# Two attentions on one core: moving A's work between steps, the first score ahead of the parts of the maximum, and some copies to other engines

## The chip, the core and the metric

The kernel runs on one core of a Trainium2 chip. The core has a matrix engine (TensorE; its matmuls are PE in the profile, its weight loads PEld), a vector engine (VectorE, DVE), a scalar engine for pointwise functions (ScalarE, ACT), a general engine (GpSimd, POOL), and SyncE (SP), which here only issues DMAs. Each engine works through its own queue in order and waits on semaphores that other engines and DMAs raise. The program writes its matmul results to eight tiles of PSUM (banks) of 128 partitions by 512 floats: seven for general use and `po`. The metric is the device time of one launch in microseconds.

## The reference

Two independent attention layers on inputs of 2048 rows and 576 columns, with 32 heads of 18 columns each; their outputs stand side by side. A attends from each position to eight earlier ones at distances 0, 2, ... 14; B attends to all positions.

```python
qkv = (x @ wqkv).reshape(B, S, 3, H, Dh).transpose(2, 0, 3, 1, 4)
# A: W, dil = 8, 2
idx = pos[:, None] - (jnp.arange(W) * dil)[None, :]
logits = einsum("bhsd,bhswd->bhsw", q, k[idx]) * Dh ** -0.5   # -1e9 where idx < 0
o = einsum("bhsw,bhswd->bhsd", softmax(logits), v[idx])
a = o.transpose(0, 2, 1, 3).reshape(B, S, D) @ wo
# B
p = softmax(einsum("bhqd,bhkd->bhqk", q, k) * Dh ** -0.5)
b = einsum("bhqk,bhkd->bhqd", p, v).transpose(0, 2, 1, 3).reshape(B, S, D) @ wo
return concatenate([a, b], axis=-1)
```

## The kernel before

**Stages.** First come the projections of B and A (up to about 412 us), which go to DRAM scratch: `dqk` and `dv` for B, `da` for A. Then the main loop at the end of the function: `NG` = 8 groups of four heads, `NB` = 4 blocks of 512 queries, `NT` = 16 tiles of 128 keys. One (g, b, kt) is a step, 512 in all; a block takes 16 steps.

**A step of B.** For four heads `score` computes a score matmul (keys by queries, 56 rows: 54 for the products and two that subtract the row's maximum) into one of four banks, and ScalarE takes the exponential into `e`. Heads 0 and 2 (h = 0, 2 in the code's order 0, 2, 1, 3) use array rows 0 to 63, heads 1 and 3 rows 64 to 127, so matmuls of the two row groups can run side by side. `weigh` (L731) multiplies the exponentials of the step before with V into `po`; after the sixteenth tile `finish` copies `po` to `o` on ScalarE (L740), and the sums are inverted and multiplied in some steps later (`den`, `drec`, `rec`).

**The maximum.** The exact maximum of each score row must be known before its block is scored. It is computed by further matmuls, pieces of it spread over all steps: `maximum(r)` does one piece of 512 columns in row group r into a bank that VectorE reduces (L168); `parts_of_maximum` does two half pieces, one of each row group, into the two halves of one bank. Both write one bank, so the program orders them: an empty ScalarE instruction (L243) stands between the two:

```python
one = both[1][0][0](ps, *both[1][1], part)
between = nc.scalar.nop()
sync(between, one)
def other():
    (take, reduce), piece = both[0]
    sync(take(ps, *piece, part), between)
    reduce(ps, *piece, part)
```

In the loop the parts come first, `other` after the third score, whole pieces after the first and the last score. These matmuls and the sums of products share three banks (`rings["else"]`). A block's maxima, transposed and split by `turn`, `halve` and `place`, are loaded into its rows of `qs` (L195) before its first score; that score is the first to wait for those loads. `given` counts pieces; when all 2048 are given, steps hold scores only and V products go in pairs of steps (`paired`).

**A beside it.** A is cut into eight tiles of 256 positions, `local(j)`, j = 0 to 7, each with a list of (step, function) from step `A_FROM + GAP * j` = 10 + 54 j: `fetch` loads q, k, v (tiles `aq`, one buffer, and `akv`, two); nine `match` on POOL multiply and add up q and k (L868, L872), the last gives the logits `lg` (L875); `most` takes the maximum over the eight neighbours on VectorE in three steps (L886), `lower` subtracts it on POOL (L892), `exponents` is on ScalarE (L895), `total` and `inverses` on VectorE, `share` multiplies on POOL (L905), and nine `weighted` on POOL (L911 to L914) make the output, which `upper` and `rest` split and `put` stores to `dao`. `get` loads it back transposed, and `sums_of_a` multiplies with wo, in four products a tile: a product is appended to `inside` at a step given by `MADE` and is issued in the next step ahead of its last score. `beside` issues it in both row groups, with two pieces of the maximum between its matmuls (L1036). `producing` holds the steps that have a product.

**Orders.** `agenda` maps a step to functions; `due()` runs a step's at its end, so what a step issues stands in its engine's queue behind that step's scores. An engine that isn't waiting may run ahead of the steps: SP and POOL do.

**The tail.** In the last group B's own products with wo (`sum_of`, L1055 and L1056) run from `waiting` in nearly every step; `closing` ends the last block.

Of the kernel before, what the change touches and what calls it, by code (L numbers as in the profile page):

```python
# [10 lines left out]
AF = mybir.ActivationFunctionType  # L11
# [8 lines left out]
DH = 18  # L20
W = 8
# [21 lines left out]
GAP = 54  # L43

A_FROM = 10

MADE = ((88, 96, 112, 128), (144, 160, 176, 192), (201, 208, 224, 240), (250, 256, 272, 288),
        (304, 320, 336, 352), (361, 368, 384, 400), (412, 416, 432, 448), (466, 468, 475, 480))


def ap(t, *dims):
# [10 lines left out]
def two_attentions(ctx: ExitStack, tc, xa, wa, woa, xb, wb, wob, out):  # L62
# [5 lines left out]
    nc = tc.nc  # L68
# [184 lines left out]
    e_room = None  # L253
    counted = [-1]

    def score(g, b, kt, h, kind="scores"):

        assert (g, b) in placed
        qs, ks = sets[g % 3]
        p, r = divmod(h, 2)  # L260
        ps = bank(kind)
        at = slice(64 * r, 64 * r + 56)
        nc.tensor.matmul(ps, ks[at, p, 128 * kt : 128 * kt + 128], qs[at, b, p], start=True, stop=True)  # L263

        counted[0] += 1
        early = counted[0] % 8 < 6
        e = (e_room if early else work).tile([128, 512], F32, name="e", bufs=6 if early else 2)
        nc.scalar.activation(e, ps, AF.Exp, scale=SCALE)  # L268
        return e
# [466 lines left out]
    def finish(g, b):  # L736
        o = work.tile([128, 512], F32, name="o", bufs=2)
        if g == NG - 1 and b == NB - 1:
            return closing(b, o, work.tile([128, 512], F32, name="rec", bufs=1))
        nc.scalar.activation(o, po, AF.Copy)  # L740
        den = work.tile([128, 16], F32, name="den", bufs=2)
        rec = work.tile([128, 512], F32, name="rec", bufs=1)
        parts = []

        def room():
            if g == NG - 1 and b == 0:

                parts[:] = [ap(work.tile([128, 4, 128], F32R, name=f"at{i}", bufs=1), (1, 512)) for i in range(2)]
            else:
                n = work.tile([128, 2, 512], F32R, name="n", bufs=1)  # L750
                parts[:] = n[:, 0], n[:, 1], n
            return parts

        if g == NG - 1 and b > 0:
            return shortly(b, o, rec, *room()[:2])

        def store():
            if g < NG - 1:
                load(do[:, g, :, 512 * b : 512 * b + 512].rearrange("i p n -> p i n"), parts[2].bitcast(F32))
            else:  # L760
                plan(step, full(b, parts))

        for at, f in ((1, lambda: load(den, o[DH:128:32])),
                      (8, lambda: nc.vector.reciprocal(den, den)),
                      (9, lambda: load(drec[g, b].rearrange("i (p n) -> (i p) n", n=16), den)),
                      (13, lambda: load(rec, rows(drec[g, b], (512, 4), (0, 32), (1, 512)))),
                      (18, lambda: nc.gpsimd.tensor_mul(o, o, rec)),  # L767
                      (19, lambda: nc.gpsimd.tensor_copy(room()[0], o)),
                      (20, lambda: nc.gpsimd.tensor_sub(parts[1], o, parts[0])),
                      (26, store)):  # L770
            later(at, f)
# [47 lines left out]
    wo = {}  # L819

    producing = set()

    def load_wo(k, src, *pieces):

# [20 lines left out]
    def local(j):  # L845
# [34 lines left out]
        def over_window(op, name, n):  # L880

            if n == 0:
                st[name] = work.tile([128, W // 2, SUB], F32, name=name, bufs=1)
            t, half = st[name], W >> n + 1
            src = t if n else st["lg"]
            nc.vector.tensor_tensor(t[:, :half], src[:, :half], src[:, half : 2 * half], op=op)  # L886

        def most(n):
            over_window(ALU.max, "am", n)
# [56 lines left out]
        def sums_of_a(h):  # L946
            his, los = zip(*wo["a"])
            w = his[:4], los[:4], his[4], los[4]
            cols = slice(288 * h, 288 * h + 288)
            if h == 0:  # L950
                st["y"] = ys["a", j, st["n"]] = work.tile([128, D], F32, name="y", bufs=4)
            one, two = beside("scores", *(halves(r, 0, w, st["x"], cols, slice(0, 128), True) for r in range(2)))
            y = st["y"][:, cols]
            nc.scalar.activation(y, two, AF.Copy)
            behind_scores.append(lambda: nc.vector.tensor_add(y, one, y))

        pieces = [(33, lower), (35, exponents), (39, share), (60, upper), (61, rest), (64, lambda: put(0)), (66, lambda: put(1))]

        pieces[:0] = [(at, lambda f=f, n=n: f(n)) for f, ats in ((most, (31, 32, 33)), (total, (36, 37, 38)),
                                                                (inverses, (38, 39))) for n, at in enumerate(ats)]  # L960
        for c in range(DH // 2):
            pieces.append((5 + 5 * c // 2, lambda c=c: match(c)))
            pieces.append((39 + 5 * c // 2, lambda c=c: weighted(c)))

        for nm, at, apart in (("q", -18, 2), ("k", -10, 2)) if j else (("q", -9, 1), ("k", -5, 1)):
            pieces += [(at + apart * i, lambda nm=nm, i=i: fetch(nm, i)) for i in range(4)]
        pieces += [(16 + 2 * i, lambda i=i: fetch("v", i)) for i in range(4)]
        made = [p - A_FROM - GAP * j for p in MADE[j]]
        for n, ends in enumerate((made[:2], made[2:])):
            pieces.append((max(ends[0] - 8, made[1] + 1 if n else 0), lambda n=n: get(n)))  # L970
            for h in range(2):
                pieces.append((ends[h], lambda h=h: finished(h)))
                producing.add(A_FROM + GAP * j + ends[h] + 1)
            pieces.append((ends[1] + 6, lambda n=n: load(out[p0 + 128 * n : p0 + 128 * n + 128, :D], ys["a", j, n])))
# [69 lines left out]
    def sum_of(y, t, h, chunks, kind=None):  # L1044

        pos, cols = slice(128 * t, 128 * t + 128), slice(288 * h, 288 * h + 288)
        both = []
        for r in range(2):
            both.append([])
            for c, (hi, lo) in enumerate(chunks):  # L1050
                at = slice(64 * r, min(64 * r + 64, hi.shape[0]))
                whi, wlo = wo["b"][c]
                both[r] += [(a[at, pos], w[at, cols]) for a, w in ((hi, whi), (hi, wlo), (lo, whi))]
        one, two = beside(kind, *both)
        nc.vector.tensor_copy(y, one)  # L1055
        nc.vector.tensor_add(y, two, y)  # L1056

    def first(t, b, h):
# [81 lines left out]
    while step < ALL:  # L1140
# [2 lines left out]
        es = [None] * 4  # L1143

        whole = total - sum(given) > 1
        parts = bool(begun) or total - sum(given) > 3

        ps = bank() if inside and whole else None
        if parts:
            part = parts_of_maximum()  # L1150
        for h in (0, 2, 1, 3):

            if inside and h == 3:
                inside.pop(0)()
            es[h] = score(g, b, kt, h)
            if h == 0 and whole:
                maximum(1, ps)()
            if h == 1 and parts:
                part()
            if h == 3 and whole:  # L1160
                maximum(0)()
        for fs in (behind_scores, outside):
# [42 lines left out]
```

## Time and profile before

| | |
|---|---|
| median of 3 runs | 1619.34 us (1617.29 to 1619.95) |
| the profiled execution | 1616.82 us, span 1615.0 us, granted TensorE clock 0.997 |
| score matmuls (L263) | 2048, 567.3 us busy |
| matmuls of the maximum (L160) | 2536, 791.8 us busy |
| products with V (L731) | 4096, 537.9 us busy |
| reductions of the maximum (L168, VectorE) | 2048, 1286.0 us busy, mean 684 ns |
| exponentials of B (L268, ScalarE) | 2048, 1050.2 us busy, mean 607 ns |
| copies of block sums (L740, ScalarE) | 31, 19.5 us busy, mean 628 ns |

A row of groups gives line, engine, operation, output and inputs, shapes and count, then busy time in us, mean ns of one, idle time of the engine just before them and what ended it. A row of the timeline gives the start, the duration, engine, line, operation, tiles, shapes and count, and in brackets the idle time before it with its releaser. A row of windows gives the stretch, its length, then busy time and count for each engine, the granted clock and the DMAs. `x2` in the timeline means that two instructions are merged into one row; the duration is then that of both.

### The profile page before, as it was taken

To read this page: it belongs to the slowest core of one execution; us is meant where nothing else is said; L and a number is where in the kernel's file an instruction comes from. 1 tells how busy PE (TensorE), PEld (TensorE's weight loads), DVE (VectorE), ACT (ScalarE), POOL (GpSimd) and SP (SyncE) were. 2 spreads that over 40 slices of the span, in tenths; PEclk is the share of its full clock that TensorE was granted. 3 is DMA by queue.
4 is the path that set the end of the run, shared out by engine and by line. 5 is a ranking of instruction groups with operands and counts; after the bars stand their busy time and mean duration, and the time that the engine had idled before them with its cause. 6 is when DMAs were issued, how large, how long until landed. Compare 5 with 4: busy or idle time off the path is not lost.

```text
span 1615.0 us, 35230 instructions
## 1 busy us (share of the span) xinstructions
PE 1599.0 (99%) x13394; PEld 959.5 (59%) x13394; DVE 1393.9 (86%) x2366; ACT 1212.4 (75%) x2419; POOL 961.1 (60%) x792
## 2 busy tenths in 40 slices
PE   9999999999999999999999999999999999999998
PEld 7999888999544444444444444444444444445676
DVE  5199999999899998999999999999999999999532
ACT  6424442121799998999999999999999999998444
POOL 2405742210265995996995995995996997920000
PEclk9999999999999999999999999999999999999999
DMA  8937954432222262254235235332532241034201
GB/s 250 239 121 196 275 164 133 134 104 79 60 56 64 73 147 54 62 118 113 62 85 133 72 98 115 98 91 60 125 106 58 59 135 47 22 124 139 89 38 60
DMA packets 186058, 172.11 MB, mean 107 GB/s; under 512 B 119152, under 2 KB 132976, under 8 KB 184160
## 3 DMA queue, kind: packets, MB, share of 16 engines
q1 hardware_dynamic: 181024, 158.31, 35.3%
q0 software_dynamic: 4032, 10.63, 3.1%
q8 instruction: 105, 1.72, 0.5%
q10 hardware_dynamic: 832, 0.92, 0.2%
q14 instruction: 65, 0.53, 0.1%
HBM read 96.94 MB, written 71.90 MB: 105 GB/s over the span
## 4 chain that ended last, share of the span: by engine, by line
PE 82%; POOL 7%; DVE 5%; DMA 3%; ACT 2%; issue 1%; SPq 0%; POOLq 0%; DVEq 0%; ACTq 0%
PE po L731 24%; PE bank L160 15%; PE bank L353 15%; PE bank L263 15%; PE bank L1036 8%; PE bank L290 5%; DVE mx L168 4%; ACT e L268 2%; POOL pr L868 1%; POOL pr L872 1%; POOL pr L911 1%; DMA akv<-da 1%; DMA dqk<-olo 1%; POOL pr L912 1%; POOL pr L913 0%
## 5 line engine op out<-in xcount | busy, mean ns | idle before, releaser
L168 DVE TENSOR_REDUCE mx<-bank 128x2 f32<-128x512 f32 x2048 | 1286.0, 684 | 114.5 <-PE bank L160 86.2
L268 ACT ACTIVATE e<-bank 128x512 f32<-128x512 f32 x2048 | 1050.2, 607 | 90.3 <-PE bank L263 83.2
L160 PE MATMUL bank<-ks,qs 54*128 54x256 f32 (+1 forms) x2536 | 791.8, 377 | 7.4 <-DVE mx L168 5.9
L160 PEld LDWEIGHTS bank<-ks,qs 54*128 54x128 f32 x2536 | 411.3, 184 | 464.6 <-DVE mx L168 423.4
L263 PE MATMUL bank<-qs,ks 56*128 56x512 f32 x2048 | 567.3, 426 | 0.1
L731 PE MATMUL po<-e,v 128*19 128x512 f32 x4096 | 537.9, 599 | 0.0
L263 PEld LDWEIGHTS bank<-qs,ks 56*128 56x128 f32 x2048 | 299.3, 185 | 14.7 <-issue 7.5
L868 POOL TENSOR_TENSOR pr<-aq,akv 128x1024 f32<-128x1024 f32 x72 | 158.5, 2202 | 15.4 <-DMA akv<-da 12.8
L911 POOL TENSOR_TENSOR pr<-lg,akv 128x1024 f32<-128x1024 f32 x72 | 158.5, 2201 | 0.6
L872 POOL TENSOR_TENSOR pr<-pr 128x1024 f32<-128x1024 f32 x64 | 152.6, 2384 | 5.0
L731 PEld LDWEIGHTS po<-e,v 128*19 128x19 f32 x4096 | 70.5, 97 | 129.4 <-issue 127.0
L681 ACT ACTIVATE ohi<-bank 128x512 f32<-128x512 f32 (+1 forms) x56 | 30.4, 595 | 152.5 <-issue 100.7
L353 PE MATMUL bank<-xhi,ahi 64*128 64x512 f32 (+1 forms) x448 | 113.5, 387 | 0.0
L353 PE MATMUL bank<-xhi,alo 64*128 64x512 f32 (+1 forms) x448 | 112.3, 387 | 0.0
L353 PE MATMUL bank<-xlo,ahi 64*128 64x512 f32 (+1 forms) x448 | 111.9, 388 | 0.1
L912 POOL TENSOR_TENSOR pr<-pr 128x512 f32<-128x512 f32 x72 | 92.5, 1285 | 5.6
L401 POOL TENSOR_TENSOR alo<-raw,ahi 128x512 fp32r<-128x512 f32 (+1 forms) x14 | 17.6, 1258 | 120.7 <-ACT ahi L400 88.8
L493 POOL TENSOR_TENSOR olo<-olo,ohi 128x512 fp32r<-128x512 f32 x36 | 46.2, 1294 | 66.1 <-ACT ohi L492 57.5
L767 POOL TENSOR_TENSOR o<-o,rec 128x512 f32<-128x512 f32 x29 | 37.6, 1297 | 58.7 <-ACT e L268 34.2
L103 POOL CAST mh<-mt 128x32 fp32r<-128x32 f32 x32 | 6.9, 217 | 102.3 <-DVE mt L183 99.5
L353 PEld LDWEIGHTS bank<-xhi,ahi 64*128 64x128 f32 (+1 forms) x448 | 65.0, 181 | 2.9
L353 PEld LDWEIGHTS bank<-xhi,alo 64*128 64x128 f32 (+1 forms) x448 | 63.9, 182 | 2.9
(197 smaller groups left out, 1827.6 us busy)
## 6 DMA issues: line engine op xcount, KB each, us to landing
do<-n SPq DMA_DIRECT2D x28, 512.0 KB
da<-ohi SPq DMA_DIRECT2D x52, 256.0 KB
akv<-da SPq DMA_DIRECT2D x64, 175.5 KB
out<-y SPq DMA_DIRECT2D x32, 288.0 KB
qs<-dqk SPq DMA_DIRECT2D x30, 288.0 KB
ks<-dqk SPq DMA_DIRECT2D x30, 288.0 KB
at<-dao SPq DMA_DIRECT2D x64, 128.0 KB
rec<-drec SPq DMA_DIRECT2D x29, 256.0 KB
```

The costliest lines, as they stand in the source:

```text
L160: return nc.tensor.matmul(ps if part is None else ps[:, 256 * r : 256 * r + 256], qs[at, b, p, 128 * t : 128 * t + 128], ks[at, p, 512 * k ...
L168: nc.vector.tensor_reduce(at, ps.rearrange("q (s n) -> q s n", s=2), axis=AX.X, op=ALU.max)
L263: nc.tensor.matmul(ps, ks[at, p, 128 * kt : 128 * kt + 128], qs[at, b, p], start=True, stop=True)
L268: nc.scalar.activation(e, ps, AF.Exp, scale=SCALE)
L290: nc.tensor.matmul(ps, a, b, start=c == i == 0, stop=c == 4 and i == 1)
L353: nc.tensor.matmul(ps, a, b, start=start, stop=stop)
L731: nc.tensor.matmul(po[32 * i : 32 * i + 19], vs[g][:, kt, 19 * i : 19 * i + 19], es[i], start=kt == 0, stop=kt == NT - 1)
L868: nc.gpsimd.tensor_mul(pr, ap(st["q"][:, 2 * c], (SUB, 2), (0, W), (1, SUB)), window(st["k"], c))
L872: nc.gpsimd.tensor_add(st["pr"], st["pr"], pr)
L911: nc.gpsimd.tensor_mul(at, ap(st["lg"], (0, 2), (SUB, W), (1, SUB)), window(st["v"], c))
L912: nc.gpsimd.tensor_add(at[:, :, :4], at[:, :, :4], at[:, :, 4:])
L1036: nc.tensor.matmul(ps, a, b, start=start, stop=stop)
```

## The change

It has seven parts. (1) In a step the first score is issued ahead of the first part of the maximum (`between`). (2) `finish` copies `po` on VectorE where the next step has no product and maxima are left; the next step then does no parts. (3) `most` and `total` work in four pieces of at most 128 elements per partition; they, `exponents`, `share`, `weighted`, `upper`, `rest` and `put` move to steps up to four later (for j = 0 four earlier than that). (4) `exponents` is issued inside a product's step where one falls on its step. (5) For j > 0 the first three matches go 15 to 18 steps ahead of the tile's start, into the step range of the tile before, the other six one or two steps earlier than they were, and q and k are fetched earlier. (6) Products of `MADE` move by up to eight steps, `get` is two steps later ahead of a product. (7) `sum_of` copies on ScalarE where its banks are both of the ring of three, in the tail.

```diff
-MADE = ((88, 96, 112, 128), (144, 160, 176, 192), (201, 208, 224, 240), (250, 256, 272, 288),
-        (304, 320, 336, 352), (361, 368, 384, 400), (412, 416, 432, 448), (466, 468, 475, 480))
+MADE = ((96, 100, 112, 128), (144, 160, 176, 192), (201, 208, 224, 240), (256, 262, 272, 288),
+        (304, 320, 336, 352), (368, 370, 384, 400), (416, 424, 432, 448), (466, 468, 475, 480))
...
-    def score(g, b, kt, h, kind="scores"):
+    def score(g, b, kt, h, kind="scores", between=None):
...
         nc.tensor.matmul(ps, ks[at, p, 128 * kt : 128 * kt + 128], qs[at, b, p], start=True, stop=True)
+        if between:
+            between()
...
-        nc.scalar.activation(o, po, AF.Copy)
+        if step + 1 in producing or sum(given) == total:
+            nc.scalar.activation(o, po, AF.Copy)
+        else:
+            nc.vector.tensor_copy(o, po)
+            copied.add(step + 1)
...
-            t, half = st[name], W >> n + 1
-            src = t if n else st["lg"]
-            nc.vector.tensor_tensor(t[:, :half], src[:, :half], src[:, half : 2 * half], op=op)
+            at, size, apart = ((0, 2, 4), (2, 2, 4), (0, 2, 2), (0, 1, 1))[n]
+            t, src = st[name], st[name] if n > 1 else st["lg"]
+            nc.vector.tensor_tensor(t[:, at : at + size], src[:, at : at + size],
+                                    src[:, at + apart : at + apart + size], op=op)
...
             y = st["y"][:, cols]
+            while beside_product:
+                beside_product.pop()()
             nc.scalar.activation(y, two, AF.Copy)
...
-        pieces = [(33, lower), (35, exponents), (39, share), (60, upper), (61, rest), (64, lambda: put(0)), (66, lambda: put(1))]
-        pieces[:0] = [(at, lambda f=f, n=n: f(n)) for f, ats in ((most, (31, 32, 33)), (total, (36, 37, 38)),
-                                                                (inverses, (38, 39))) for n, at in enumerate(ats)]
-        for c in range(DH // 2):
-            pieces.append((5 + 5 * c // 2, lambda c=c: match(c)))
-            pieces.append((39 + 5 * c // 2, lambda c=c: weighted(c)))
-        for nm, at, apart in (("q", -18, 2), ("k", -10, 2)) if j else (("q", -9, 1), ("k", -5, 1)):
+        soon = 0 if j else 4
+        in_product = A_FROM + GAP * j + 36 - soon in MADE_IN
+        pieces = [(34, lower), (36, (lambda: beside_product.append(exponents)) if in_product else exponents),
+                  (43, share), (64, upper), (65, rest), (68, lambda: put(0)), (70, lambda: put(1))]
+        pieces[:0] = [(at, lambda f=f, n=n: f(n)) for f, ats in ((most, (31, 32, 33, 34)), (total, (38, 39, 40, 41)),
+                                                                (inverses, (42, 43))) for n, at in enumerate(ats)]
+        pieces += [(43 + 5 * c // 2, lambda c=c: weighted(c)) for c in range(DH // 2)]
+        pieces = [(at - soon, f) for at, f in pieces]
+        pieces += [(5 + 5 * c // 2 if not j else (-18, -17, -15)[c] if c < 3 else 11 + 5 * (c - 3) // 2, lambda c=c: match(c))
+                   for c in range(DH // 2)]
+        for nm, at, apart in (("q", -26, 2), ("k", -25, 2)) if j else (("q", -9, 1), ("k", -5, 1)):
...
-            pieces.append((max(ends[0] - 8, made[1] + 1 if n else 0), lambda n=n: get(n)))
+            pieces.append((max(ends[0] - 6, made[1] + 1 if n else 0), lambda n=n: get(n)))
...
-        nc.vector.tensor_copy(y, one)
+        if kind:
+            nc.vector.tensor_copy(y, one)
+        else:
+            nc.scalar.activation(y, one, AF.Copy)
         nc.vector.tensor_add(y, two, y)
...
-        parts = bool(begun) or total - sum(given) > 3
+        parts = (bool(begun) or total - sum(given) > 3) and step not in copied
         ps = bank() if inside and whole else None
-        if parts:
-            part = parts_of_maximum()
+        part = []
         for h in (0, 2, 1, 3):
...
-            es[h] = score(g, b, kt, h)
+            es[h] = score(g, b, kt, h, between=(lambda: part.append(parts_of_maximum())) if parts and h == 0 else None)
             if h == 0 and whole:
                 maximum(1, ps)()
             if h == 1 and parts:
-                part()
+                part[0]()
```

More of the change, by code (lines that the diff above doesn't have):

```diff
@@ L821, in two_attentions @@
     producing = set()
+    copied = set()
+    MADE_IN = {p for ends in MADE for p in ends}
+    beside_product = []
     def load_wo(k, src, *pieces):
```

## The prediction

> **What bounds the kernel now.** I read the page first, for the engines' shares and the chain that ended last, then a step of the main loop in the timeline, then windows over the loop.
>
> ```profile
> span 1615.0 us, 35230 instructions
> ...
> PE 1599.0 (99%) x13394; PEld 959.5 (59%) x13394; DVE 1393.9 (86%) x2366; ACT 1212.4 (75%) x2419; POOL 961.1 (60%) x792
> ...
> PE 82%; POOL 7%; DVE 5%; DMA 3%; ACT 2%; issue 1%; SPq 0%; POOLq 0%; DVEq 0%; ACTq 0%
> ```
>
> TensorE is on the path nearly everywhere. The chain also says that POOL is on it somewhere (7%). One ordinary step, with no product of A in it:
>
> ```profile
> 898.92 0.38 PE L160 MATMUL bank<-ks,qs 54*128 54x256 f32 x1
> 898.93 0.49 PE L263 MATMUL bank<-qs,ks 56*128 56x512 f32 x1
> 899.03 0.30 PEld L263 LDWEIGHTS bank<-qs,ks 56*128 56x128 f32 x2
> 899.15 0.40 PE L160 MATMUL bank<-ks,qs 54*128 54x512 f32 x1
> 899.26 0.52 PE L263 MATMUL bank<-qs,ks 56*128 56x512 f32 x2
> 899.41 0.18 PEld L160 LDWEIGHTS bank<-ks,qs 54*128 54x128 f32 x1
> 899.50 0.29 PE L160 MATMUL bank<-ks,qs 54*128 54x256 f32 x1
> 899.58 1.89 DVE L168 TENSOR_REDUCE mx<-bank 128x2 f32<-128x512 f32 x3 [0.18 <-PE bank L160]
> 899.96 1.05 PE L731 MATMUL po<-e,v 128*19 128x512 f32 x8
> 900.94 0.38 PE L160 MATMUL bank<-ks,qs 54*128 54x256 f32 x1
> ```
>
> The matmuls run in two row groups side by side: the first part of the maximum (898.92, 256 columns, group 1) with the first score (898.93, 512 columns, group 0), and so on; then the eight products with V (899.96), and the next step begins at 900.94, after 2.02 us. The reader should see a small wait in the middle. The second part (899.50) goes into the same bank as the first, so the program puts an empty ScalarE instruction (L243) between them: it waits for the first part, and the second part waits for it. The first part ends at 898.92 + 0.38 = 899.30; the weights of the second are loaded from 899.41, 0.11 later, while the weight loader has been idle since 899.33. So **each step already hangs on part 1, ScalarE, part 2**, at present almost for free, because row group 0 is busy with the score of 899.26 until about then.
>
> ```profile
> L243 ACTq EVENT_SEMAPHORE  x488: 17/17/17, 418.8 to 1504.8; - x163
> 700.90:727.35 26.45, 14.45 (x52) 7.70 (x52) 1.00 0.69 146
> 418.30:1498.00 1079.70, 546.90 (x1944) 288.49 (x1944) 1.00 0.34 89
> 418.30:1498.00 1079.70, 75.74 (x864) 69.69 (x864) 1.00 0.34 89
> 1264.10 0.38 PE L160 MATMUL bank<-ks,qs 54*128 54x256 f32 x1
> 1268.24 0.38 PE L160 MATMUL bank<-ks,qs 54*128 54x256 f32 x1
> ```
>
> The first row counts that instruction: 488 steps have one. The window rows are of the scores (L263, four a step) and of A's products (L1036, 27 matmuls each). 52 scores in 26.45 us is 2.035 us a step. A step with a product takes 1268.24 - 1264.10 = 4.14 us, 2.11 more. The loop from 418.30 to 1498.00 has 1944 / 4 = 486 steps and 864 / 27 = 32 products: 486 x 2.035 + 32 x 2.11 = 1056.5. It took 1079.7, so **23 us in it are stalls**: the most that better placing can win there. The rest is the rate of the step.
>
> **The change part by part.**
>
> *First score ahead of part 1.* No instruction is added. But the part is now the second matmul in TensorE's queue, behind a longer one in the other row group. If a matmul's signal leaves at its own end, that is free. If signals leave in program order, the part's can't come before the score's. One place of the trace tells, in the stage of the projections:
>
> ```profile
> 88.83 0.50 PE L160 MATMUL bank<-ks,qs 54*128 54x512 f32 x1
> 88.83 0.39 PE L353 MATMUL bank<-whh,xhl 64*128 64x288 f32 x1
> 89.40 0.29 ACT L571 ACTIVATE vs<-bank 128x144 f32<-128x144 f32 x1 [4.22 <-PE bank L160]
> ```
>
> ScalarE, idle for 4.22 us, waits only for the product whose last matmul is the short one (288 columns, done at 89.22). It starts at 89.40, 0.07 after the end of the long one that was queued ahead of it (89.33), and the view names the long one as releaser. An ordinary release takes 0.03 (899.15 + 0.40 to 899.58). So the short one's signal followed the long one's by some 0.04: program order.
>
> Here that means: part 1 signals not 0.38 us after the start, but at the score's 0.49 plus 0.04, that is 0.15 later. ScalarE's empty instruction, the weights of part 2 and all of TensorE behind them move by as much, since its queue is in order. Part 2 would start at 0.58 + 0.15 = 0.73. What follows it takes 900.94 - 899.50 = 1.44, and no less where it is late already:
>
> ```profile
> 449.42 0.38 PE L160 MATMUL bank<-ks,qs 54*128 54x256 f32 x1
> 449.78 0.47 PE L263 MATMUL bank<-qs,ks 56*128 56x512 f32 x1
> 450.32 0.28 PE L160 MATMUL bank<-ks,qs 54*128 54x256 f32 x1
> 451.75 0.38 PE L160 MATMUL bank<-ks,qs 54*128 54x256 f32 x1
> 452.21 0.63 ACT L740 ACTIVATE o<-po 128x512 f32<-128x512 f32 x1
> 456.27 0.38 PE L160 MATMUL bank<-ks,qs 54*128 54x256 f32 x1
> 1480.76 0.38 PE L160 MATMUL bank<-ks,qs 54*128 54x256 f32 x1
> 1481.16 0.46 PE L263 MATMUL bank<-qs,ks 56*128 56x512 f32 x1
> ```
>
> At 449.42 part 2 came 0.90 after part 1 and the next step began 451.75 - 450.32 = 1.43 after it: lateness of part 2 passes on whole. The new step is 0.73 + 1.43 = 2.16, 0.12 over 2.035. Bounds: nothing (own end) and 0.15 (no absorption). I take 0.12, as the row at 89.40 is of the same engine and the same pairing of row groups. The first score doesn't reach ScalarE earlier either: its exponential is queued behind the empty instruction. Number of steps: 488, less six that skip their part (below), and two late steps that get one back: 484 x 0.12 = **+58 us** (0 to 73).
>
> [...]
>
> The same edit also gains. At 449.42 and 1480.76, steps that open a new block of queries, the score starts 0.36 and 0.40 after the part instead of beside it, as it first waits for several loads into qs. With the score first, these waits run during the products with V before it. Of the 31 block openings about a dozen show it, the two rows being the first and last: 12 x 0.36 = -4.3.
>
> *VectorE copies the block sums.* The copy on ScalarE (452.21) stretches the two steps around it to 456.27 - 451.75 = 4.52, 0.45 over two plain ones. Six copies have no product behind them (steps 16 to 80 and 464). On VectorE it queues behind three reductions and the next V products wait for it: I leave 0.2 each, so -1.5 (0 to -2.7). The part that is skipped pays for the VectorE time; its six pieces of the maximum come back in steps 488 to 490, where two products then take pieces between their matmuls: some +0.6 there, which I set against fewer waits. 0.
>
> *A's chain, its matches and loads.*
>
> ```profile
> 622.61 0.43 DVE L886 TENSOR_TENSOR am<-lg 128x256 f32<-128x256 f32 x1 [3.38 <-POOL lg L875]
> 623.68 0.58 PE L160 MATMUL bank<-ks,qs 54*128 54x256 f32 x1 [2.85 <-DVE mx L168]
> 623.60:630.70 7.10, 7.01 (x45) 5.04 (x45) 5.25 (x11) 2.69 (x5) 0.00 (x0) 0.54 0.19 47
> L868 POOL TENSOR_TENSOR pr<-aq,akv 128x1024 f32<-128x1024 f32 x72 | 158.5, 2202 | 15.4 <-DMA akv<-da 12.8
> L872 POOL TENSOR_TENSOR pr<-pr 128x1024 f32<-128x1024 f32 x64 | 152.6, 2384 | 5.0
> L892 POOL TENSOR_TENSOR lg<-lg,am 128x512 f32<-128x512 f32 x8 | 10.3, 1282 | 38.8 <-DVE am L886 38.8
> L905 POOL TENSOR_TENSOR lg<-lg,as 128x512 f32<-128x512 f32 x8 | 10.2, 1279 | 60.3 <-DVE as L902 53.3 <-ACT e L268 7.1
> ```
>
> The one large stall is in the second tile: VectorE's maximum stood 3.38 us at POOL's logits, TensorE idled 2.85, and then ran 7.1 us at a granted clock of 0.54, which costs 7.1 x 0.46 = 3.3: 6 together. Three matches of the next tile cost 3 x 2.20 + 2 x 2.38 = 11.4 us of POOL and go into its idle time at the chain, (38.8 + 60.3) / 8 = 12.4 us a tile, so POOL comes to the logits earlier; and the first product moves from step 88 to 96, behind it in part. -6 (0 to -6). The chain's pieces of 256 elements (0.43) become two of half the size: a little more VectorE work, in smaller pieces over four more steps. The exponentials go beside a product in five of the eight tiles. For these and all other stalls 23 - 6 - 4.3 - 6 x 0.45 = 10 are left. By the new places alone I would give 1.5 of them back; with steps of 2.16 VectorE and ScalarE have 0.12 more in each step, and I leave 3.5: -6.5 (-9 to +2). The loads: q and k of the next tile are issued some 10 and 15 steps earlier. On SP they stand ahead of the sums' small loads and wait for POOL's last match to free aq; nothing on TensorE's path stands behind them within a few steps. 0. The fetch for a product is issued six steps ahead, not eight, and the tile's stores four steps later: 0 while it lands within six steps, 12 us (a rival below).
>
> *ScalarE in the tail.* There TensorE runs a product in every step:
>
> ```profile
> 1592.46 0.46 DVE L1055 COPY y<-bank 128x288 f32<-128x288 f32 x1 [3.55 <-PE bank L1036]
> 1592.69 2.07 ACT L268 ACTIVATE e<-bank 128x512 f32<-128x512 f32 x4 [0.32 <-PE bank L263]
> 1595.17 0.62 PE L731 MATMUL po<-e,v 128*19 128x512 f32 x4
> ```
>
> The copy is as long on ScalarE, and pushes the four exponentials by 0.2, to 1594.98, still before 1595.17. 0 (-1 to +2).
>
> **Sum** against the profiled execution (1616.8, span 1615.0): +58 - 4.3 - 1.5 - 6 - 6.5 = +40. A little of the gains is lost since the stalls no longer give the other engines time to catch up: +38. The median shown is 2.5 above that execution: 1619.3 + 38 = **1657**.
>
> **Rivals.**
> 1. *Signals leave at each matmul's own end.* Then part 1 signals at 0.38 as now, and the gains stand alone: -4.3 - 1.5 - 6, and only -1.5 of A's chain: -13, **1606**. For it: the row at 89.40 is a single place, of another stage. Against: the view names the long matmul as releaser there. It decides from a delay of part 2 under 13 / 484 = 0.03. Chance 0.11.
> 2. *The delay is mostly absorbed*, because steps wait in that time for other things anyway. Left 0.04 x 484 = 19, against 17 of gains: **1621**. Against: 1.43 after a late part 2. Chance 0.05.
> 3. *Forecast, and a product finds its data late* (tiles 4 and 7, whose products stay while the stores move back): a stall as at 623.68, some 6 us: **1663**. Chance 0.06; slower steps speak against it, as they leave the loads more time.
> 4. *The forecast*, **1657**: 0.78.
>
> **Numbers.** The per-step cost from 0.09 to 0.15 gives 44 to 73; the recovered stalls 14 to 24: 1639 to 1676. I take 1637 to 1678, which leaves out rivals 1 and 2. A measurement tells 0.2% (3 us) from no change: faster 0.11, same 0.05, slower 0.84.
>
> **What would show it.** Right: part 2 starts 0.73 after its step's first matmul, plain steps take 2.15 (52 scores in 28 us), the score of a new block starts with its step, no stall at the second tile, the clock near 1.0, shares of DVE and ACT lower over a longer span. Wrong: part 2 still at 0.58, then it is rival 1; part 2 at 0.73 but steps of 2.05, rival 2.

## The result and the profile after

The changed kernel took 1661.92 us (median of 4 runs, 1661.38 to 1662.10), the kernel before 1618.32 us beside it (4 runs, 1615.92 to 1619.95): a ratio of 1.0272, 95% interval 1.0255 to 1.0288. The forecast was 1657 (1637 to 1678). In the changed kernel the score is L263, its exponential L270, the products with V L733, A's products L1057, matches L879 and L883, the logits L886, VectorE's window operations L898, the share L918.

First the page of the kernel after: span, engines, the chain that ended last, and two groups, whose last columns are the idle time ahead of it and what ended it.

```profile
span 1660.0 us, 35220 instructions
...
PE 1648.0 (99%) x13390; PEld 943.0 (57%) x13390; DVE 1395.8 (84%) x2361; ACT 1231.4 (74%) x2440; POOL 962.0 (58%) x792
...
PE 93%; DVE 2%; DMA 2%; POOL 1%; issue 1%; SPq 1%; ACT 0%; POOLq 0%; ACTq 0%; DVEq 0%
...
L263 PEld LDWEIGHTS bank<-qs,ks 56*128 56x128 f32 x2048 | 304.4, 184 | 423.5 <-ACT e L270 415.6
...
L160 PEld LDWEIGHTS bank<-ks,qs 54*128 54x128 f32 x2532 | 398.2, 184 | 114.2 <-ACTq L243 99.5
```

On the page of the kernel before, the same two groups:

```profile
L160 PEld LDWEIGHTS bank<-ks,qs 54*128 54x128 f32 x2536 | 411.3, 184 | 464.6 <-DVE mx L168 423.4
...
L263 PEld LDWEIGHTS bank<-qs,ks 56*128 56x128 f32 x2048 | 299.3, 185 | 14.7 <-issue 7.5
```

VectorE and GpSimd work as long as before and ScalarE 19 us longer, in a span 45 us longer; the chain is nearly all TensorE's (93%, 82% before). The row of L160 names the new wait: 99.5 us in which the weight loader stood idle until ScalarE's empty instruction L243. (The idle time of some 420 us, 0.85 at the start of each step, while the products with V run, only changes rows, as the step now opens with the score.) One plain step in the timeline shows it:

```profile
897.59 0.50 PE L263 MATMUL bank<-qs,ks 56*128 56x512 f32 x1
...
898.23 0.18 PEld L160 LDWEIGHTS bank<-ks,qs 54*128 54x128 f32 x1 [0.22 <-ACTq L243]
898.23 0.39 PE L160 MATMUL bank<-ks,qs 54*128 54x256 f32 x1
...
899.75 0.49 PE L263 MATMUL bank<-qs,ks 56*128 56x512 f32 x1
```

The weights of the second part start 0.64 us after the step's first matmul (before: 899.41 - 898.92 = 0.49), and the step takes 899.75 - 897.59 = 2.16. The windows of the scores (stretch, length, busy time and count) give it for many steps, 52 scores and then the loop:

```profile
672.00:700.08 28.08, 14.72 (x52) 7.78 (x52) 1.00 0.09 30
418.50:1544.00 1125.50, 559.99 (x1944) 293.21 (x1944) 1.00 0.34 85
```

The first stretch holds 52 scores, 13 steps at 2.160 us. The loop's 486 steps took 1125.5 us, 45.8 more than before. 486 x (2.160 - 2.035) = +60.8; so the stalls shrank by 15.0. With 32 products at 2.11 (a step with a product still takes 2.10 us more than a plain one, 4.26 in the median), what is left in the loop beside the plain rate is 1125.5 - 486 x 2.160 - 67.5 = 8.2 us, where it was 23.

### The profile page after: what moved, and what is told of

Read it like the earlier page. It is cut to its first block, busy times and chain, and to the rows that moved or that the text cites. A ratio compares the mean times of both kernels' runs of the same rounds, so it can differ in the third digit from the quotient of the medians.

```text
span 1660.0 us, 35220 instructions
## 1 busy us (share of the span) xinstructions
PE 1648.0 (99%) x13390; PEld 943.0 (57%) x13390; DVE 1395.8 (84%) x2361; ACT 1231.4 (74%) x2440; POOL 962.0 (58%) x792
## 4 chain that ended last, share of the span: by engine, by line
PE 93%; DVE 2%; DMA 2%; POOL 1%; issue 1%; SPq 1%; ACT 0%; POOLq 0%; ACTq 0%; DVEq 0%
PE po L733 29%; PE bank L263 20%; PE bank L160 18%; PE bank L355 14%; PE bank L1057 7%; PE bank L292 5%; DVE mx L168 1%; DMA ks<-dqk 1%; POOL xlo L403 1%; DMA at<-dao 1%; DMA dqk<-olo 0%; DVE as L898 0%; SPq L143 0%; PE bank L507 0%; DMA more<-xa 0%
## 5 line engine op out<-in xcount | busy, mean ns | idle before, releaser
L270 ACT ACTIVATE e<-bank 128x512 f32<-128x512 f32 x2048 | 1061.7, 605 | 95.3 <-PE bank L160 40.1
L160 PE MATMUL bank<-ks,qs 54*128 54x256 f32 (+1 forms) x2532 | 836.2, 390 | 2.6 <-DVE mx L168 2.0
L263 PE MATMUL bank<-qs,ks 56*128 56x512 f32 x2048 | 581.5, 429 | 0.0
L263 PEld LDWEIGHTS bank<-qs,ks 56*128 56x128 f32 x2048 | 304.4, 184 | 423.5 <-ACT e L270 415.6
L733 PE MATMUL po<-e,v 128*19 128x512 f32 x4096 | 537.6, 599 | 0.2 <-DVE o L746 0.2
L160 PEld LDWEIGHTS bank<-ks,qs 54*128 54x128 f32 x2532 | 398.2, 184 | 114.2 <-ACTq L243 99.5
L879 POOL TENSOR_TENSOR pr<-aq,akv 128x1024 f32<-128x1024 f32 x72 | 158.3, 2203 | 53.4 <-DMA akv<-da 32.1
L883 POOL TENSOR_TENSOR pr<-pr 128x1024 f32<-128x1024 f32 x64 | 152.5, 2383 | 5.0
L733 PEld LDWEIGHTS po<-e,v 128*19 128x19 f32 x4096 | 70.5, 97 | 130.6 <-issue 125.2
L355 PE MATMUL bank<-xlo,ahi 64*128 64x512 f32 (+1 forms) x448 | 117.1, 388 | 0.1
L355 PEld LDWEIGHTS bank<-xlo,ahi 64*128 64x128 f32 (+1 forms) x448 | 67.4, 182 | 4.9 <-POOL xlo L403 0.5
```

The source lines that it names most:

```text
L160: return nc.tensor.matmul(ps if part is None else ps[:, 256 * r : 256 * r + 256], qs[at, b, p, 128 * t : 128 * t + 128], ks[at, p, 512 * k ...
L355: nc.tensor.matmul(ps, a, b, start=start, stop=stop)
L733: nc.tensor.matmul(po[32 * i : 32 * i + 19], vs[g][:, kt, 19 * i : 19 * i + 19], es[i], start=kt == 0, stop=kt == NT - 1)
L879: nc.gpsimd.tensor_mul(pr, ap(st["q"][:, 2 * c], (SUB, 2), (0, W), (1, SUB)), window(st["k"], c))
L883: nc.gpsimd.tensor_add(st["pr"], st["pr"], pr)
```

## The experiments

The theory: the step's lengthening is the late signal of part 1. A rival for the sum: the rest of the change costs something, too. The first four runs part them. "Score first alone" is the kernel before with `between` and nothing else; "part first again" is the kernel after without it.

```diff
 # e2, e4 against the kernel after (e4: only where kt == 0 and not 96 <= step < 368 is the score first)
-        part = []
+        part = [parts_of_maximum()] if parts else []
...
-            es[h] = score(g, b, kt, h, between=...)
+            es[h] = score(g, b, kt, h)
 # e3 against the kernel after, in steps that hold whole pieces and no product
-            if h == 1 and parts:
-                part[0]()
+            if h == 1: maximum(0)()      # it stood behind the fourth score
...
+        part[0]()                                      # behind the fourth score
+        rings["else"].append(rings["else"].pop(0))
```

> The kernel before with one thing of the change alone: the first score ahead of the first part of the maximum in every step. Theory (TensorE's signals leave in program order, so the part's signal now leaves behind the longer score's, and the second part, which waits for it through ScalarE's empty instruction, starts 0.12 to 0.13 us later in each of some 488 steps): 488 x 0.125 = +61 us, less the block-opening waits of some 4 us that go with it, so about 1675 us (1665 to 1682), plain steps of 2.16 us, and the stall of some 6 us in the second tile is still there. Rival (the rest of the change, A's chain and the copies, costs the time, and each signal leaves at its own end): 1605 to 1620 us, plain steps of 2.03 us.

> The changed kernel with this one thing undone: the first part of the maximum stands ahead of the first score again; A's chain at its new steps, the block sums by VectorE and ScalarE in the tail stay. Theory: the plain step is 2.03 us again, 61 us go, the block-opening waits of some 4 us come back, and what is left is the rest of the change against the kernel before: 1605 to 1614 us, with the stall of the second tile gone and the two late products of tiles 2 and 3 (steps 225 and 269 to 273) still there or a little worse, since the steps are shorter. Rival (the rest of the change costs something too): above 1620 us, up to 1650.

> The changed kernel with the first score still in front, but in the steps without a piece of a product the second part of the maximum goes to the end of the step, behind the last whole maximum and the last score; its signal is then long there when its turn comes. In the steps with a piece of a product the order of the changed kernel is kept. Theory (what costs is the wait for the late signal in the middle of the step, not the place of the score): plain steps of 2.03 to 2.06 us, weight loads of the second part without idle time before them, and some 430 of the 484 steps get their 0.125 us back: 1661 - 54 = 1607 us (1603 to 1618). Rival (a score in front costs TensorE 0.12 us in itself, by the pairing of the row groups): plain steps stay at 2.16 us and the time at 1650 to 1662 us. A third reading: the third bank of the ring comes free later, and the parts wait for VectorE instead: between the two.

> The changed kernel with the score in front of the part only in the step that opens a block (21 steps or so, outside blocks 3 to 11 of which the first chain's tiles don't allow it), and the part in front in all other steps. Theory: the gain of the score in front sits in these steps alone, some 0.3 us each where a block's load of the maxima or its exponential was waited for, and its price in all the others: 2 to 4 us below the kernel with the part first everywhere (1603 to 1611 us). Rival (the opening waits are only moved to the next matmul in the step): no difference from the kernel with the part first everywhere, within 1 us.

| kernel | us | ratio to before, 95% |
|---|---|---|
| before, beside these four | 1616.78 | |
| e1, score first alone | 1657.01 | 1.0248 (1.0220 to 1.0276) |
| e2, all of the change but that | 1632.26 | 1.0097 (1.0074 to 1.0119) |
| e3, second part last | 1641.92 | 1.0156 (1.0131 to 1.0181) |
| e4, score first at openings | 1628.35 | 1.0074 (1.0050 to 1.0097) |

**The score in front alone costs 40 us, and the rest of the change 15 us without it.** Neither number is what I expected: e1 came out 18 below its 1675, e2 18 above its range. The loops, in windows of the scores, e1 and then e2:

```profile
418.18:1539.25 1121.07, 558.87 (x1944) 292.76 (x1944) 1.00 0.33 86
```

```profile
418.66:1514.35 1095.69, 546.25 (x1944) 288.96 (x1944) 0.99 0.35 87
```

With steps of 2.160, e1 has 1121.1 - 1049.8 - 67.5 = 3.8 us of stalls left of the 23, and none in the second tile (tile 1, as tiles are numbered from 0). My reading is that steps 0.12 longer give the other engines the time that they lacked. There GpSimd's logits are done before VectorE asks for them (e1, timeline):

```profile
625.59 1.28 POOL L877 TENSOR_TENSOR lg<-pr 128x512 f32<-128x512 f32 x1
...
627.80 0.42 DVE L888 TENSOR_TENSOR am<-lg 128x256 f32<-128x256 f32 x1
```

The logits end at 626.87 and VectorE comes at 627.80, without idle time; in the kernel before it stood 3.38 us at this place. A's chain hasn't moved in e1. The control of e6, below, bears the reading out without any change of order: its steps are 0.03 us longer than before, and at this place TensorE stands 1.30 us in place of 2.85. And e2, at 2.035, has 1095.7 - 989.0 - 67.5 = 39 us of stalls, 16 more than before.

**e3** gave half an answer. Its steps alternate; the timeline over two of them, with the first score of each step and the weights of its second whole maximum:

```profile
949.56 0.50 PE L263 MATMUL bank<-qs,ks 56*128 56x512 f32 x1
...
949.98 0.18 PEld L160 LDWEIGHTS bank<-ks,qs 54*128 54x128 f32 x1
...
951.56 0.50 PE L263 MATMUL bank<-qs,ks 56*128 56x512 f32 x1
...
952.16 0.18 PEld L160 LDWEIGHTS bank<-ks,qs 54*128 54x128 f32 x1
...
953.76 0.50 PE L263 MATMUL bank<-qs,ks 56*128 56x512 f32 x1
```

One step takes 2.00 us with the score in front, so its place costs TensorE nothing in itself. The next takes 2.20: these weights come 0.60 after the step's start, not 0.42, since VectorE has only then freed the bank (its reduction ends at 952.10). That is the third reading. The time, between the two theories, doesn't part them; the steps of 2.00 do.

**e6 and its control** test the signal itself: the first score in two halves, so that a matmul of its own length stands ahead of the part.

```diff
 # both, against the kernel before; e6 only: between() after c == 0
+            for c in range(2):
+                nc.tensor.matmul(ps[:, 256 * c : 256 * c + 256], ks[...],
+                                 qs[at, b, p, 256 * c : 256 * c + 256], start=True, stop=True)
+                if between and c == 0:
+                    between()
```

> The kernel before, with each step's first score as two matmuls of 256 columns, the first part of the maximum behind the first of them. To be read against its control, which has the same two halves and the part ahead of both. Theory (the part's signal waits for the end of what stands ahead of it in the program, here a matmul of its own length, not for one of twice the columns): the second part's weights start at 0.49 to 0.55 us after the step's first matmul, and the plain step is 0 to 0.06 us longer than the control's. Rival (whatever stands ahead in the other row group costs the same, by its being there): 0.12 us longer, as with the whole score.

> The control: the kernel before with the first score of each step as two matmuls of 256 columns and nothing else. Both theories: the price of one more matmul and weight load in a step alone, 0 to 0.06 us in each of 512 steps, 1617 to 1650 us, and the second part's weights at 0.48 us after the step's first matmul as in the kernel before.

1624.86 us (1.0044, 1.0027 to 1.0061) and 1627.70 us for the control (1.0066, 1.0047 to 1.0085). The weight loader, e6 and then the control: the step's first weights and those of its second part.

```profile
899.13 0.18 PEld L160 LDWEIGHTS bank<-ks,qs 54*128 54x128 f32 x1
...
899.65 0.18 PEld L160 LDWEIGHTS bank<-ks,qs 54*128 54x128 f32 x1
```

```profile
897.92 0.18 PEld L160 LDWEIGHTS bank<-ks,qs 54*128 54x128 f32 x1 [0.85 <-DVE mx L168]
...
898.41 0.18 PEld L160 LDWEIGHTS bank<-ks,qs 54*128 54x128 f32 x1
```

0.52 against 0.49: a score of equal length ahead of the part delays it by 0.03, not 0.15. The median step without a product is 2.07 us in both, and the whole run isn't longer than its control. The rival, which asked for 60 us, is out: what costs is that the part's signal waits for the end of a *longer* matmul queued ahead of it. The traces show the signal itself, in the start of the empty instruction that waits for it: in the median of the steps that have one it comes 0.42 us after the start of part 1 in the kernel before and in the control, 0.45 in e6 and 0.56 in the kernel after and in e1. Before the change that is 0.04 behind the end of part 1; with it, 0.18 behind that end and 0.07 behind the end of the score.

**Where A's chain costs.** Of the large new stalls in e2, those at steps 46, 103, 157 and 374 lie where VectorE adds up the exponentials. The timeline of e2 at step 103, in three engines:

```profile
638.35 2.37 POOL L883 TENSOR_TENSOR pr<-pr 128x1024 f32<-128x1024 f32 x1
638.54 2.33 DVE L898 TENSOR_TENSOR as<-lg 128x128 f32<-128x128 f32 x1
640.79 1.88 DVE L168 TENSOR_REDUCE mx<-bank 128x2 f32<-128x512 f32 x3
640.80 2.18 POOL L879 TENSOR_TENSOR pr<-aq,akv 128x1024 f32<-128x1024 f32 x1
...
642.12 0.38 PE L160 MATMUL bank<-ks,qs 54*128 54x256 f32 x1 [1.90 <-DVE mx L168]
```

An addition that takes 0.28 us at its shortest takes 2.33. It starts just behind GpSimd's 2.37 us addition for the *next* tile's matches and ends at 640.87, 0.15 after that one. VectorE's reductions queue behind it, the banks come free late, TensorE stands 1.90 us. Before the change GpSimd was idle there. Two runs try this cause: e5 (and e7, with the openings) moves the early matches away, e11 leaves them and gives VectorE's maxima and sums one input in place of two.

```diff
 # e5 against e2, e7 against e4
-        pieces += [(5 + 5 * c // 2 if not j else (-18, -17, -15)[c] if c < 3 else 11 + 5 * (c - 3) // 2, ...
+        pieces += [(5 + 5 * c // 2, ...
 # e11 against e2
-            nc.vector.tensor_tensor(t[:, at : at + size], src[:, at : at + size],
-                                    src[:, at + apart : at + apart + size], op=op)
+            at = SUB // 4 * n
+            nc.vector.tensor_reduce(st[name][:, 0, at : at + SUB // 4],
+                                    st["lg"][:, :, at : at + SUB // 4].rearrange("p w s -> p s w"), axis=AX.X, op=op)
```

> The kernel with the part first everywhere and the rest of the change (1632 us), and all matches of a tile back at the steps of the kernel before (5 + 5c/2 behind the tile's start), so none of the next tile's matches lies beside VectorE's sums and ahead of the tile's weighted pieces on GpSimd; the fetches stay early. Theory (the first three matches, moved ahead, keep GpSimd busy while VectorE adds the exponents, so that VectorE's additions of 0.28 us take up to 2.3 us, the ends of GpSimd's instructions set theirs, and VectorE's reductions and TensorE's banks come late; and they stand in front of the share on GpSimd while k is still being fetched, so that the products of tiles 2 and 3 wait for data): the stalls at steps 46, 103, 157, 258 and 374 (15 us) and the wait at step 225 (8.6 us) go, no sum of VectorE above 1.3 us, 1608 us (1603 to 1616). Rival (the later steps of the chain and the earlier fetches cost it, not the matches): 1626 to 1634 us.

> The same edit of the matches in the kernel with the score in front at the openings of the blocks alone (1628 us): with the theory 1605 us (1600 to 1613), below the kernel before by 0.4 to 1%, and 2 to 4 us below the one with the part first everywhere; with the rival 1622 to 1630 us.

> The kernel with the part first everywhere and the rest of the change (1632 us), with VectorE's maxima and sums over the window as reductions of one input, four quarters of 32 columns at the same four steps, in place of four additions with two inputs each. GpSimd's matches stay where they are. Theory (VectorE's additions of two inputs wait for the end of GpSimd's multiplication or addition, and a reduction of one input doesn't): no sum above 0.6 us, the stalls at steps 46, 103, 157, 258 and 374 (15 us together) fall below 5 us, the wait for data at step 225 stays: 1618 to 1625 us. Rival (any operand of VectorE in SBUF waits beside GpSimd, or the stalls come from the number of VectorE's instructions): sums up to 2.3 us and 1629 to 1636 us as before.

e5 took 1676.96 us (1.0381, 1.0354 to 1.0408), e7 1672.91 us (1.0340, 1.0321 to 1.0359): both far off, in a way that neither theory had. The waits of e5 (who waits for whom; us in total, times, longest) say why:

```profile
DVE am L898 <- POOL lg L886: 40.9, 6, 9.2
```

The longest sum is 0.63 us now, but the logits are late: in six tiles VectorE stands at them, up to 9.2 us. Each tile ends on GpSimd four steps later than in the kernel before, and without an early start the next tile's nine matches don't fit behind it. The early matches are not the mistake of the change; they pay for its four steps.

e11 took 1623.25 us (1.0037, 1.0024 to 1.0049), 9.0 below e2, in the range expected. The groups of the sums of shares in e2 and e11 (min, median, max in ns):

```profile
L898 DVE TENSOR_TENSOR as<-lg x16: 281/460/2326, 510.8 to 1379.8; 128x128 f32<-128x128 f32 x16
```

```profile
L895 DVE TENSOR_REDUCE as<-lg x32: 362/373/380, 511.1 to 1375.1; 128x16 f32<-128x128 f32 x32
```

With GpSimd's matches where they were, no sum takes over 0.38 us, and the four stalls are down to 0.5 us and less (step 258, which I had counted among them, is a wait for logits and keeps 1.6). So the wait came with VectorE's additions of two inputs beside GpSimd's instructions: up to 2.33 us against 0.28 in e2, and 0.36 to 0.38 with the reductions of one input in e11.

**The rest.** e8 is the kernel after with A's chain of the kernel before; e9 has that chain, the openings, the copies and the tail.

> The changed kernel with A's chain as in the kernel before (its matches, its maxima and sums, its fetches, the steps of its products), and the rest of the change kept: score in front of the part everywhere, block sums copied by VectorE, ScalarE in the tail. Theory (A's chain at its new steps costs some 5 us beside long steps, the copies and the tail bring 1 to 3 us): 1652 to 1657 us, the sums of VectorE at 0.2 to 0.5 us again, and no product that waits for data. Rival (the copies by VectorE or ScalarE's part in the tail cost what the score in front alone doesn't): 1659 to 1664 us.

> The kernel before with A's chain as it was, the score in front of the part only in the step that opens a block, block sums copied by VectorE and ScalarE in the tail. Theory: the openings give 3 to 4 us, the copies and the tail 2 to 3 us, the stall of 6 us in the second tile stays: 1609 to 1614 us, below the kernel before by 0.2 to 0.5%. Rival (what the openings gain is waited for elsewhere): 1616 to 1619 us.

e8: 1656.57 us (1.0247, 1.0233 to 1.0261). Against the kernel after, 5.3 less in the medians (4 by the ratios, 6 in the loop): that is what A's new chain costs beside long steps. Against e1, 0.4 less: beside long steps, copies and tail together bring nothing that the times can tell.

e9: 1625.66 us (1.0055, 1.0041 to 1.0068) where 1609 to 1614 was expected: a miss. Tile 5, which had got by, doesn't any more (timeline of e9):

```profile
1031.76 1.28 POOL L773 TENSOR_TENSOR o<-o,rec 128x512 f32<-128x512 f32 x1 [9.09 <-DMA rec<-drec]
...
1106.52 1.26 POOL L882 TENSOR_TENSOR lg<-pr 128x512 f32<-128x512 f32 x1
...
1107.81 1.47 DVE L893 TENSOR_TENSOR am<-lg 128x256 f32<-128x256 f32 x1 [6.17 <-POOL lg L882]
...
1110.53 0.58 PE L160 MATMUL bank<-ks,qs 54*128 54x256 f32 x1 [7.29 <-DVE mx L168]
```

In the kernel before, the same logits had been just in time, ready at 1100.21 and taken at 1102.81:

```profile
1098.92 1.29 POOL L875 TENSOR_TENSOR lg<-pr 128x512 f32<-128x512 f32 x1
...
1102.81 0.96 DVE L886 TENSOR_TENSOR am<-lg 128x256 f32<-128x256 f32 x1
```

The step itself starts only 1.3 us earlier in e9; the logits are 7.6 us later. GpSimd had lost that time 75 us before, at the multiplication of a block's sums of B (1031.76), where it stood 9.09 us for the load of the inverted sums; in the kernel before it ran the same one at 1024.19 without waiting. SyncE issued that load at 1019.35, not at 1011.58, and its queue had been 6.5 us late since the loads of B's split maxima (983.34, not 976.84). Those wait for GpSimd's splitting, which in e9's queue stands behind the last match and the logits of tile 4, and before the change ahead of both. The order probably comes from the steps that skip their part, which leave each block's maxima complete a step later; no run shows that.

**The late products.** e2's largest stall, and one of e11's, is a product that waits for its data (step 225). In e11's timeline it can be followed back through three queues, GpSimd, SyncE, TensorE:

```profile
885.41 4.36 POOL L879 TENSOR_TENSOR pr<-aq,akv 128x1024 f32<-128x1024 f32 x2 [18.55 <-DMA den<-o]
...
898.82 2.30 SPq L195 DMA_DIRECT2D qs<-mh  x4
898.87 0.25 POOL L104 TENSOR_TENSOR mt<-mt,mh 128x32 fp32r<-128x32 f32 x1
...
903.92 0.93 SPq L946 DMA_DIRECT2D at<-dao  x2
...
906.96 0.54 PE L1054 MATMUL bank<-wohi,at 64*128 64x288 f32 x2 [2.21 <-DMA at<-dao]
```

GpSimd stands 18.55 us at tile 4's first match, which reads only q and k, so I take it that it waits for its k (the view names another transfer); behind the match stands the splitting of B's maxima, behind that SyncE's loads of them, and behind those the fetch of the product. The last run moves this match behind the share and adds the openings.

```diff
 # e12 against e11, beside e4's edit
-        ... (-18, -17, -15)[c] if c < 3 else ...
+        ... (-9, -8, -6)[c] if c < 3 and j in (4, 5) else (-18, -17, -15)[c] if c < 3 else ...
```

> The kernel with the one-input sums (1623 us), with two things more: the score in front of the part in the steps that open a block (outside blocks 3 to 11), and the three early matches of tiles 4 and 5 at 9, 8 and 6 steps ahead of the tile in place of 18, 17 and 15, so that GpSimd issues the share of the tile before them and doesn't stand with its queue full behind a match that waits for its k. Theory (the waits for data at steps 225 and 273, 6.4 and 7.2 us, come from that match: behind it GpSimd's splitting of the maxima is late, behind that SyncE's loads, behind those the product's): both waits go, the openings give 3 to 4 us: 1605 us (1601 to 1611), below the kernel before by 0.4 to 0.9%. Rival (these products wait for their transfers beside the loads of the stacks, whatever GpSimd does): both waits stay and the time is 1617 to 1621 us.

1622.03 us (1.0032, 1.0022 to 1.0041). The wait at step 225 is gone and that at 273 is 0.7 us, so the cause was right. But the 18 us don't come. GpSimd stands nearly as long as in e11, now at the multiplication of B's sums that had stood behind the match; tile 4's matches come after that, VectorE stands at its logits and TensorE with it, and then TensorE runs slowly (timeline of e12, then a window of TensorE, whose last numbers are the granted clock and the DMAs):

```profile
883.01 1.28 POOL L774 TENSOR_TENSOR o<-o,rec 128x512 f32<-128x512 f32 x1 [17.87 <-DMA out<-y]
...
983.99 0.37 DVE L895 TENSOR_REDUCE am<-lg 128x16 f32<-128x128 f32 x1 [6.80 <-POOL lg L886]
...
985.61 0.58 PE L160 MATMUL bank<-ks,qs 54*128 54x256 f32 x1 [6.52 <-DVE mx L168]
```

```profile
985.60:993.00 7.40, 7.39 (x44) 0.70 0.30 63
```

6.5 us idle and 7.4 x 0.30 = 2.2 us of clock; step 305, with another product that waits for its data, is 7.3 us longer than its like. No version of mine beats the kernel before; the best two are 0.3 and 0.4% slower.

## Why the prediction was right, and where it wasn't

**The bound and the step.** Right. The signals left in program order here: e6 shows it by a score of equal length (0.03 us later), the start of the empty instruction by a signal that is 0.14 us later (0.15 forecast), and the steps of 2.00 in e3 show that the score's place alone costs nothing. The term was +58 (484 x 0.12); measured +60.8 in the loop (486 x 0.125), and e1 shows that it comes from this one edit.

**"Part 2 would start at 0.58 + 0.15 = 0.73."** Wrong in its detail: it started at 0.64. Before, the matmul of part 2 ran 0.09 behind its weights (899.41 and 899.50), since row group 0 was still busy; after, weights and matmul start together. The weights did move by 0.15 (0.49 to 0.64), and what follows the matmul takes 1.52 in place of 1.44. The two errors cancel: 2.16, as forecast.

**The stalls, -4.3 - 1.5 - 6 - 6.5 = -18.3.** The size was near, -15.0 in the loop, and that was in part luck, as the cause of about half of it was wrong. I gave -6 to the new places of A's chain in the second tile, and -6.5 to A's chain and longer steps together. e1, with the chain unmoved, has 3.8 us of stalls left: the longer steps (with the openings) recover 19. The new chain takes 6 of them back (e8: 1119.4 - 1049.8 - 67.5 = 2.1 us left; after: 8.2). At the old step length the new chain, with the copies and the tail, cost 15 us (e2). The window of e8's loop:

```profile
418.70:1538.05 1119.35, 556.85 (x1944) 291.93 (x1944) 1.00 0.34 86
```

I had said of the three early matches only that they go into GpSimd's idle time. That VectorE adds up the exponentials in that time, and that its additions of 0.28 us take up to 2.33 beside them (e2), I didn't ask.

**Copies and tail.** I took -1.5 and 0. Together they bring 0.4 in the medians (e8 against e1), too little to measure. The longer step had already taken what the copies were to save: around the six blocks, three steps together were 0.4 to 0.6 us over plain ones before the change, and with the copy still on ScalarE, in e1, 0.0 to 0.2.

**The last steps of the sum.** +40 became +38 because "a little of the gains is lost". A lost gain makes the time longer, so by its own reason it should have become +42, or 1661. And 1619.3 + 73 - 14 is 1678, not 1676, as the range that was given has it.

**Rivals.** 1 and 2 fell with the first row of the result. 3 (a product finds its data late) did happen, and not where I put it: not through stores four steps later in tiles 4 and 7, but in tiles 2 and 3, by a match in front of the fetch, three queues away. In the kernel after it is 2.2 us, 1.1 at each of steps 225 and 273. I had argued that longer steps leave the loads more time, and with shorter ones the first of them is 8.6 us (e2).

**What stays open.** Whether the openings are worth anything by themselves. Their wait was read rightly: in the kernel before the first scores of 30 blocks came 4.3 us behind their parts in all, and in e1 each opens its step. But e4 lies 3.9 us under e2, but its own nine runs go from 1623 to 1636. That GpSimd's share of a tile could be made to fit with steps of 2.03 wasn't tried.

## What to carry to other kernels

Where an engine waits for one matmul of a pair that runs side by side, queue the short one first: here, with the longer score ahead, ScalarE's instruction that waits for the part started 0.56 us after the part's start and not 0.42, and a step took 2.16 us in place of 2.035. Gains of a few us from moving work "into idle time" have to be checked against which other engine's instructions slow down beside the moved one (VectorE's additions in e2, 0.28 to 2.33 us), and against what stands behind it in its queue, two or three queues on; and a kernel whose step is set by one engine can hide its stalls when that step gets longer (in e1 3.8 us of 23 were left), so a term read as "recovered by the change" may be recovered by the slowdown.

## What the runs showed of the hardware

VectorE's long additions of two operands beside GpSimd ended with GpSimd's instruction: the five sums above 1 us in e2 end 0.14 to 0.15 us after it, the longest at 2.33 us for 0.28, and the three in the kernel after (1.38, 1.49 and 1.99 us) 0.09 to 0.15 us after it. The reductions with one operand in their place took 0.36 to 0.38 us in e11. And TensorE's clock fell after an idle time of 1.90 us: in e2 the 5.6 us behind it ran at 0.70, 1.7 us more for 1.9 of waiting. In the same run it fell for 3.4 us behind idle times of 1.68, 1.70 and 1.95 us too; behind 1.54 us in e11 (step 258) it did not.

```profile
642.10:647.70 5.60, 5.58 (x32) 0.70 0.13 45
```
